# Sines left in PSUM, and a gating whose products run on GpSimd and whose sums run on VectorE in PSUM

## The chip, the cores and the metric

The kernel runs on one core of one Trainium2 chip. A core has five engines with a queue each: TensorE (PE in the profile; its weight loads are shown apart, as PEld), VectorE (DVE), ScalarE (ACT), GpSimd (POOL) and SyncE (SP, which here only issues DMAs). The two on-chip memories are SBUF and PSUM; PSUM is used here as eight banks of 128 x 512 fp32. The metric is the device time of one execution in microseconds (us); lower is better. Everything is fp32.

## The reference

`x` is (1, 2048, 512). Four layers are added to it in turn, A, B, A, B, each on a layer norm of `x` over the channels:

```python
def A(q, k, v, shift_k, ssm_k, ssm_D):            # q is the normalized x
    k_shift = sum(k_pad[:, t:t+S] * shift_k[:, 3-t] for t in range(4))
    kv = k_shift * v                              # the gating: the same in both A layers
    y = causal_conv(kv, ssm_k) + kv * ssm_D       # FFT of length 2S, per channel
    return q * y

def B(u, log_A_real, A_imag, C_real, C_imag, log_dt, D_skip):
    dt = exp(log_dt);  A = -exp(log_A_real) + 1j * A_imag;  C = (C_real + 1j * C_imag) * dt
    K = 2 * real(sum_n C[d, n] * exp(A[d, n] * dt[d] * l))      # the taps, l = 0 .. 2047
    return causal_conv(u, K) + u * D_skip

x = x + A(layernorm(x));  x = x + B(layernorm(x))
x = x + A(layernorm(x));  x = x + B(layernorm(x))
```

`kv` and its convolution don't depend on `x`, so the kernel computes the convolution of A once. It also computes the taps of B once.

## The kernel before

**The stages.** After a short setup (the logarithms, phases and rates of the modes, lines 330 to 424), two generators are run together by `run_steps`: one step of `stream()`, then two of `diagonal()`, again and again.

- `stream()` makes the taps of B (`taps`, 64 steps, four to each of 16 groups of 32 channels) and, behind them, the spectrum of B's filter (`spectrum_quarter(1, ...)`).
- `diagonal()` makes the spectrum of A's filter (four quarters of 12 steps). With each of these steps it runs one step of `kv_steps`, which is the gating: 16 groups of 32 channels, three steps a group, by `gated`. Then it runs the convolution of A (`convolution(0, ...)`), which reads the gated groups back from DRAM (`kv_d`).

When both are done, `gated_update` multiplies `x` by A's result, the first B convolution runs, then the second gated update and the second B convolution. None of these last parts is touched by the change.

**One step of the taps.** A tap is a product of a magnitude and a wave, and each is split into two factors, so that 32 x 64 positions come out of a contraction over the modes.
- `mags` (line 469): TensorE writes log magnitudes to a bank `pm`, ScalarE takes Exp of it into SBUF (L471): `m1` (512 columns a step) and `m2` (512 columns every second step). Twelve Exps are made for eight steps at a time, because Exp and Sin need different activation tables.
- `angles`: TensorE writes a phase in turns into a bank `pa` (L481; there are two such banks), VectorE rounds it (`y`, L485), TensorE subtracts the rounded phase in the same bank (L486).
- `waves`: ScalarE reads `pa` and writes to the SBUF tile `tt` (three of them): the absolute value (L494), the sine (L495), and the cosine from the absolute value (L496).
- `products`, one step later: GpSimd makes L507 (sine and cosine times `m1`, 2 x 8 x 32 columns) and L511 (cosine, 8 x 32 columns). VectorE makes L508 (sine and cosine times `m2`, in place in `tt`, 2 x 8 x 32 columns) and L509 (minus the sine times `m1`, 8 x 32 columns). All operands are in SBUF.
- `contract` (L522): 32 small matmuls add the products up in the bank `pk`; every fourth step VectorE scales the result (L531, L532) and SyncE stores it.

**One group of the gating.** `gated` loads a tile `kvt` (19 rows of k, 16 of v, the four shift weights), and does eight elementwise operations of 128 x 512 on it, all in SBUF: VectorE makes L621, L625, L628, L629, GpSimd L622, L623, L626, L630 (the bits of `KVE`). They form one chain of sums `u`, which goes back and forth between the two engines; `u` is stored to `kv_d` by L631. Group 0 is made on GpSimd alone. The tiles `u` and `tb` share the tags `vv` and `sw` (two buffers each) with the convolution of A.

**PSUM.** In this part of the kernel the eight banks are: one `pk`, two `pa`, two `pm`, and three of the tag `c1`, which the forward transforms (`pf`, L171), the spectrum (`pu`, L196), and the convolution of A (`pi`, `po`) take in turn. The SBUF tag `pc` has two buffers: the spectrum of A copies a bank `pu` there by ScalarE (L247) and stores it to DRAM (L248).

**What sets the order.** The program is written in the order above, but `TileContext(schedule_with_timeline_sim=True)` lets a planner choose the order on each engine when the program is built, from its own modelled times. Each engine then works through its queue in that order and waits where an operand or a buffer isn't ready.

Of the kernel before, what the change touches and what calls it, by code (L numbers as in the profile page):

```python
# [24 lines left out]
TWO_PI = 6.283185  # L25
# [74 lines left out]
def kernel(ctx: ExitStack, tc: tile.TileContext, out, x_in, kv_in, ssmk_in, ssmd_in,  # L100
# [336 lines left out]
    NT = 3  # L437
    tts = []
    for i in range(NT):
        tt = wk.tile([128, 2, 8, 65], F32, name=f"tt{i}")  # L440
        G.memset(tt[:, 0, :, 0], 1.0)
        G.memset(tt[:, 1, :, 0], 0.0)
        tts.append(tt)


    rows, ms, xys, pks, angs = {}, {}, {}, {}, {}
    NXY = 2
    NM1 = 9
    NM2 = 5
    E2P = 1000  # L450
    XLP = 1000
    last_exp, last_sin = [None], [None]
# [11 lines left out]
    def mags(gi, k, col):  # L464
        h, s = divmod(k, 2)
        hs = slice(64 * h, 64 * h + 64)
        pm = pp.tile([128, 512], F32, name="pm", tag="pm", bufs=NPM)
        rhs = tabs["tg2"][hs] if col == 2 else tabs["tg1"][hs, 8 * s:8 * s + 8, :]
        mt = T.matmul(pm, rows[gi][hs, 1, :], rhs, start=True, stop=True)  # L469
        m = wk.tile([128, 512], F32, name=f"m{col}", tag=f"m{col}", bufs=NM2 if col == 2 else NM1)  # L470
        i = S.activation(m, pm, AF.Exp)  # L471
        if last_sin[0] is not None:
            after(i, last_sin[0])
        last_exp[0] = i
        ms[gi, k, col] = m

# [12 lines left out]
    def waves(gi, k):  # L489
        r = angs[gi, k]  # L490
        tt = tts[(4 * gi + k) % NT]
        rv = r.rearrange("p (c i) -> p c i", i=64)
        co = tt[:, 0, :, 1:65]
        S.activation(co, rv, AF.Abs)  # L494
        for i in (S.activation(tt[:, 1, :, 1:65], rv, AF.Sin, scale=TWO_PI),  # L495
                  S.activation(co, co, AF.Sin, scale=-TWO_PI, bias=halfpi)):  # L496
            after(i, last_exp[0])
            last_sin[0] = i

    def products(gi, k):  # L500
        h, s = divmod(k, 2)
        tt = tts[(4 * gi + k) % NT]
        m1 = ms[gi, k, 1].rearrange("p (c i) -> p c i", i=64)
        m2 = ms[gi, 2 * h, 2].rearrange("p (c i) -> p c i", i=32)[:, 8 * s:8 * s + 8, :]
        xy = wk.tile([128, 2, 8, 64], F32, name="xy", tag="xy", bufs=NXY)
        e2 = tt[:, :, :, 33:65]
        G.tensor_mul(xy[:, :, :, 32:64], tt[:, :, :, 1:33], m1[:, :, 32:64][:, None].to_broadcast([128, 2, 8, 32]))  # L507
        (G if (4 * gi + k) % E2P == E2P - 1 else V).tensor_mul(e2, e2, m2[:, None].to_broadcast([128, 2, 8, 32]))  # L508
        V.scalar_tensor_tensor(xy[:, 1, :, 0:32], tt[:, 1, :, 0:32], -1.0, m1[:, :, 0:32],  # L509
                               op0=ALU.mult, op1=ALU.mult)  # L510
        (V if (4 * gi + k) % XLP == XLP - 1 else G).tensor_mul(xy[:, 0, :, 0:32], tt[:, 0, :, 0:32], m1[:, :, 0:32])  # L511
        xys[gi, k] = (xy, e2)

    def contract(gi, k):
        xy, e2 = xys[gi, k]
# [86 lines left out]
    with ExitStack() as actx:  # L602
# [9 lines left out]

        def gated(grp, onpool):
            kvt = ap.tile([128, 39, 32], F32, name="kvt", tag="kab", bufs=NKA)
            nc.sync.dma_start(kvt.rearrange("p t c -> p (t c)"), kv_in[grp])
            u = ap.tile([128, 16, 32], F32, name="u", tag="vv", bufs=NSA)
            tb = ap.tile([128, 16, 32], F32, name="tb", tag="sw", bufs=NSA)
            e = [G if (onpool >> i) & 1 else V for i in range(8)]
            sk = lambda j: kvt[:, 35 + j, :][:, None, :].to_broadcast([128, 16, 32])
            kt = lambda j: kvt[:, j:j + 16, :]  # L620
            e[0].tensor_mul(u, kt(3), sk(0))  # L621
            e[1].tensor_mul(tb, kt(0), sk(3))  # L622
            e[2].tensor_add(u, u, tb)  # L623
            yield
            e[3].tensor_mul(tb, kt(1), sk(2))  # L625
            e[4].tensor_add(u, u, tb)  # L626
            yield
            e[5].tensor_mul(kt(2), kt(2), sk(1))  # L628
            e[6].tensor_add(u, u, kt(2))  # L629
            e[7].tensor_mul(u, u, kt(19))  # L630
            nc.sync.dma_start(kv_d[grp], u.rearrange("p t c -> p (t c)"))  # L631
            yield

        KV0 = 1
        KVE = 0b10010110
        def row_stats(t):
# [4 lines left out]
        def kv_steps():  # L641
            for grp in range(KV0, 16):
                yield from gated(grp, KVE)

# [26 lines left out]
        def diagonal():  # L671
            kvs = kv_steps()
            for q in range(NQ):
                for i, _ in enumerate(spectrum_quarter(0, q, ssmk_in, ap, zlast, ZA, "c1")):
                    if q == 0 and i == 1:
                        for grp in range(KV0):
                            for _ in gated(grp, 255):
                                pass
# [272 lines left out]
```

## Time and profile before

| | |
|---|---|
| device time, median of 3 runs | 789.33 us (789.06 to 796.64) |
| span of the profiled execution | 792.0 us, first to last instruction; a time of its own isn't listed beside it |
| PE, DVE busy over the span | 638.7 us (81%), 605.1 us (76%) |
| POOL, ACT busy over the span | 499.9 us (63%), 482.4 us (61%) |
| first and last gating product L630 | 30.0 us, 229.5 us |
| first and last product L507 of the taps | 71.3 us, 509.2 us |
| mean granted clock of TensorE | 0.882 |

The span falls into five stretches: setup (to about 55 us), taps with gating and A's spectrum (55 to 230), taps with the convolution of A (230 to 430), the last taps with the first gated update (430 to 512), and the B convolutions with the second gated update (from 512). The change touches the first four.

How to read the lines of the profile: a line of a group reads `line engine operation out<-in shape xcount | busy us, mean ns | idle before, and what ended it`. A line of one source line gives `duration ns min/median/max`. A line of the timeline gives the start and the duration in us.

### The profile page before, as it was taken

The page shows a single profiled execution, that of the slowest core. Times are in us where ns is not written, and L with a number is a line of the kernel's source. Part 1 is how long each engine was busy: PE and PEld are TensorE (multiplying, and loading weights), DVE is VectorE, ACT ScalarE, POOL GpSimd, SP SyncE. Part 2 cuts the span into 40 slices and gives each one's busy share as a digit, 9 for nine tenths or more (in the row PEclk, how much of TensorE's full clock was granted, in tenths as well). Part 3 has the DMA queues.
Part 4 walks back from the last instruction along what each step waited for, and adds up shares of the span by engine and source line. Part 5 has one row for each costly group of instructions (what it writes and reads, how often), then busy time and mean ns, then how long its engine had stood idle before and what let it go on. Part 6 is the DMA issues. An engine that isn't in the chain of part 4 may idle for free.

```text
span 792.0 us, 14443 instructions
## 1 busy us (share of the span) xinstructions
PE 638.7 (81%) x5064; PEld 450.9 (57%) x5064; DVE 605.1 (76%) x957; ACT 482.4 (61%) x870; POOL 499.9 (63%) x478
## 2 busy tenths in 40 slices
PE   3368697878779988998989885689779963699996
PEld 2255465546567665766757453476647731376673
DVE  7757979998984769657767849745659889968775
ACT  5035356354448695586686598748746638669572
POOL 4865778776858786665778423315766830488793
PEclk9676599678989999999999976599989995999998
DMA  9677167367457464556473591147977631077782
GB/s 324 199 245 276 44 233 254 114 201 258 135 179 199 130 163 129 146 167 183 113 202 116 156 310 71 27 137 202 241 193 211 161 95 65 1 187 228 197 246 101
DMA packets 80396, 135.47 MB, mean 171 GB/s; under 512 B 8508, under 2 KB 29508, under 8 KB 78788
## 3 DMA queue, kind: packets, MB, share of 16 engines
q1 hardware_dynamic: 79428, 132.13, 55.9%
q0 software_dynamic: 896, 2.43, 1.1%
q8 instruction: 40, 0.66, 0.4%
q14 instruction: 32, 0.26, 0.1%
HBM read 98.87 MB, written 35.65 MB: 170 GB/s over the span
## 4 chain that ended last, share of the span: by engine, by line
PE 27%; DVE 11%; ACT 8%; issue 7%; DMA 5%; POOL 3%; SPq 0%; DVEq 0%; POOLq 0%; ACTq 0%
PE pu L196 9%; PE pf L171 6%; PE pi L293 6%; PE po L314 4%; DMA kab<-spec 3%; DVE x L737 2%; ACT tt L494 1%; DMA spec<-pc 1%; PE pm L469 1%; PE pk L522 1%; DVE w L308 1%; DVE xy L509 1%; DVE vv L281 1%; POOL sw L283 1%; ACT m L471 1%
## 5 line engine op out<-in xcount | busy, mean ns | idle before, releaser
L283 POOL TENSOR_TENSOR sw<-sw,kab 128x512 f32<-128x512 f32 x96 | 125.1, 1309 | 70.2 <-ACT sw L280 57.6
L507 POOL TENSOR_TENSOR xy<-tt,m 128x512 f32<-128x512 f32 x64 | 86.4, 1351 | 71.6 <-ACT tt L496 45.5
L171 PE MATMUL pf<-kk,wz 128*128 128x256 f32 x256 | 89.8, 500 | 36.8 <-POOL kk L239 24.8
L281 DVE TENSOR_TENSOR vv<-pu,kab 128x512 f32<-128x512 f32 x96 | 64.8, 680 | 64.9 <-ACT sw L280 35.9
L293 PE MATMUL pi<-vv,mm 128*128 128x128 f32 x768 | 106.5, 283 | 3.1 <-DVE vv L281 1.6
L284 POOL TENSOR_TENSOR vv<-vv,sw 128x512 f32<-128x512 f32 x76 | 99.5, 1313 | 14.1 <-DVE vv L281 11.0
L293 PEld LDWEIGHTS pi<-vv,mm 128*128 128x128 f32 x768 | 95.8, 195 | 16.7 <-issue 8.6
L279 ACT ACTIVATE sw<-pu 64x512 f32<-64x512 f32 x96 | 57.1, 595 | 72.2 <-PE pu L196 70.4
L171 PEld LDWEIGHTS pf<-kk,wz 128*128 128x128 f32 x256 | 60.0, 249 | 56.9 <-POOL kk L239 27.6
L494 ACT ACTIVATE tt<-pa 128x512 f32<-128x512 f32 x64 | 38.3, 599 | 82.4 <-PE pa L486 73.8
L196 PE MATMUL pu<-x,w 128*128 128x128 f32 x512 | 79.3, 306 | 10.7 <-DVE x L191 9.3
L196 PEld LDWEIGHTS pu<-zu,w 128*128 128x128 f32 x512 | 63.4, 193 | 40.0 <-DVE vv L281 15.8
L196 PEld LDWEIGHTS pu<-x,w 128*128 128x128 f32 x512 | 72.3, 215 | 22.6 <-DVE x L191 12.4
L196 PE MATMUL pu<-zu,w 128*128 128x128 f32 x512 | 73.1, 285 | 10.4 <-DVE vv L281 10.1
L508 DVE TENSOR_TENSOR tt<-tt,m 128x512 f32<-128x512 f32 x64 | 73.3, 1145 | 3.4 <-ACT tt L496 3.1
L247 ACT COPY pc<-pu 128x512 f32<-128x512 f32 x64 | 37.5, 592 | 55.0 <-PE pu L196 35.2
L509 DVE SCALAR_TENSOR_TENSOR xy<-tt,m 128x256 f32<-128x256 f32 x64 | 52.7, 824 | 23.2 <-ACT tt L495 12.3
L471 ACT ACTIVATE m<-pm 128x512 f32<-128x512 f32 x96 | 54.0, 604 | 21.2 <-PE pm L469 20.1
L522 PE MATMUL pk<-xy,tt 128*32 128x64 f32 x2048 | 51.6, 240 | 13.7 <-POOL xy L511 8.1
L314 PE MATMUL po<-w,w 128*64 128x512 f32 x192 | 54.9, 662 | 8.5 <-DVE w L308 6.8
L191 DVE STREAM_TRANSPOSE x<-pf 128x512 f32<-128x512 f32 x64 | 44.8, 704 | 20.3 <-PE pf L171 20.3
L522 PEld LDWEIGHTS pk<-xy,tt 128*32 128x32 f32 x2048 | 38.0, 121 | 38.8 <-issue 16.9
(146 smaller groups left out, 1310.9 us busy)
## 6 DMA issues: line engine op xcount, KB each, us to landing
kab<-spec SPq DMA_DIRECT2D x188, 256.0 KB, 4.0
spec<-pc SPq DMA_DIRECT2D x64, 256.0 KB, 2.1
kvt<-kv_in SPq DMA_DIRECT2D x16, 624.0 KB
yaq<-ya_d SPq DMA_DIRECT2D x8, 1024.0 KB, 7.1
kk<-ssmk_in SPq DMA_DIRECT2D x16, 256.0 KB, 3.1
kv_d<-u SPq DMA_DIRECT2D x16, 256.0 KB, 7.3
kdram<-ks SPq DMA_DIRECT2D x64, 64.0 KB, 1.9
kk<-kdram SPq DMA_DIRECT2D x16, 256.0 KB, 2.9
```

The source lines that it names most:

```text
L171: yield T.matmul(o, w, rhs, start=True, stop=True)
L196: ins = T.matmul(pu[:, i, :], w2[:, c * CK + i, :], z[:, :, c * CK + i, :], start=True, stop=True)
L281: V.tensor_mul(vv, pu, kabs[s][:, 0])
L283: (V if last else G).tensor_mul(sw, sw, kabs[s][:, 1])
L284: (V if last or s % add_dve == add_dve - 1 else G).tensor_add(vv, vv, sw)
L293: i1s[t] = T.matmul(pi[:, i, :], mm[:, c * CK + i, :], vvs[t][:, i, :], start=True, stop=True)
L314: ins = T.matmul(po[64 * a:64 * a + 64], w4, ws[g][:, :, 16 * a:16 * a + 16, :].rearrange("p x t r -> p t x r"), start=True, stop=True, ti ...
L471: i = S.activation(m, pm, AF.Exp)
L507: G.tensor_mul(xy[:, :, :, 32:64], tt[:, :, :, 1:33], m1[:, :, 32:64][:, None].to_broadcast([128, 2, 8, 32]))
L508: (G if (4 * gi + k) % E2P == E2P - 1 else V).tensor_mul(e2, e2, m2[:, None].to_broadcast([128, 2, 8, 32]))
L509: V.scalar_tensor_tensor(xy[:, 1, :, 0:32], tt[:, 1, :, 0:32], -1.0, m1[:, :, 0:32], op0=ALU.mult, op1=ALU.mult)
L522: T.matmul(pk[32 * i4:32 * i4 + 32, 2 * k + i, :], e2[:, r, 4 * i + i4, :], xy[:, r, 4 * i + i4, :], start=r == 0, stop=r == 1, tile_posit ...
```

## The change

**Taps.** The sine is no longer written to SBUF: ScalarE writes it over the phase in the bank `pa`. Only the cosine goes to SBUF, to `co`. The four products become: GpSimd makes both products with the cosine (512 and 256 columns), and VectorE both with the sine, which it reads from PSUM (512 and 248 columns). `m1` and `m2` lie side by side in one tile `m` of 16 x 96 columns, so one product covers a factor with `m1` and one with `m2`. The results go to `xye`, which holds the two factors of the contraction (two tiles, used in turn; its one column that stays zero is set once).

**Gating.** GpSimd makes the four products of shifted k and shift weight (`term`, in the tags `vv` and `sw`). ScalarE copies the first into a bank `acc` of the tag `c1`, VectorE adds the other three to it in PSUM, and multiplies by v into a tile `un`, which takes a buffer of the tag `pc` and is stored from there. Group 0 is made in the same way. The three steps of a group stay three: two products, two products, the rest.

```diff
     def mags(gi, k, col):
-        m = wk.tile([128, 512], F32, name=f"m{col}", tag=f"m{col}", bufs=NM2 if col == 2 else NM1)
-        i = S.activation(m, pm, AF.Exp)
+        if col == 2:
+            ms[gi, h] = wk.tile([128, 16, 96], F32, name="m", tag="m", bufs=NM)     # NM = 5
+            m = ms[gi, h][:, :, 64:96]
+        else:
+            m = ms[gi, h][:, 8 * s:8 * s + 8, 0:64]
+        i = S.activation(m, pm.rearrange("p (c i) -> p c i", c=16 if col == 2 else 8), AF.Exp)
     def waves(gi, k):
+        rv = angs[gi, k].rearrange("p (c i) -> p c i", i=64)
+        co = cosines[(4 * gi + k) % NT][:, :, 1:65]
         S.activation(co, rv, AF.Abs)
-        for i in (S.activation(tt[:, 1, :, 1:65], rv, AF.Sin, scale=TWO_PI),
+        for i in (S.activation(rv, rv, AF.Sin, scale=TWO_PI),
                   S.activation(co, co, AF.Sin, scale=-TWO_PI, bias=halfpi)):
     def products(gi, k):
-        G.tensor_mul(xy[:, :, :, 32:64], tt[:, :, :, 1:33], m1[:, :, 32:64][:, None].to_broadcast([128, 2, 8, 32]))
-        (G if (4 * gi + k) % E2P == E2P - 1 else V).tensor_mul(e2, e2, m2[:, None].to_broadcast([128, 2, 8, 32]))
-        V.scalar_tensor_tensor(xy[:, 1, :, 0:32], tt[:, 1, :, 0:32], -1.0, m1[:, :, 0:32],
-        (V if (4 * gi + k) % XLP == XLP - 1 else G).tensor_mul(xy[:, 0, :, 0:32], tt[:, 0, :, 0:32], m1[:, :, 0:32])
+        si = angs[gi, k].rearrange("p (c i) -> p c i", i=64)
+        co = cosines[(4 * gi + k) % NT]
+        m = ms[gi, h][:, 8 * s:8 * s + 8, :]
+        xye = factors[(4 * gi + k) % NXY]                                           # NXY = 2
+        G.tensor_mul(xye[:, 0, :, 32:96], co[:, :, 1:65], m[:, :, 32:96])
+        V.tensor_mul(xye[:, 1, :, 32:96], si, m[:, :, 32:96])
+        V.scalar_tensor_tensor(xye[:, 1, :, 1:32], si[:, :, 0:31], -1.0, m[:, :, 1:32],
+        G.tensor_mul(xye[:, 0, :, 0:32], co[:, :, 0:32], m[:, :, 0:32])
     def contract(gi, k):
-                    T.matmul(pk[32 * i4:32 * i4 + 32, 2 * k + i, :], e2[:, r, 4 * i + i4, :],
-                             xy[:, r, 4 * i + i4, :], start=r == 0, stop=r == 1,
+                    T.matmul(pk[32 * i4:32 * i4 + 32, 2 * k + i, :], xye[:, r, 4 * i + i4, 64:96],
+                             xye[:, r, 4 * i + i4, 0:64], start=r == 0, stop=r == 1,
...
-        def gated(grp, onpool):
+        def gated(grp):
-            e[0].tensor_mul(u, kt(3), sk(0))
-            e[1].tensor_mul(tb, kt(0), sk(3))
-            e[2].tensor_add(u, u, tb)
-            yield
-            e[3].tensor_mul(tb, kt(1), sk(2))
-            e[4].tensor_add(u, u, tb)
+            for j, tag in enumerate(("vv", "sw", "vv", "sw")):
+                term = ap.tile([128, 16, 32], F32, name="term", tag=tag, bufs=NSA)  # NSA = 2
+                G.tensor_mul(term, kvt[:, 3 - j:19 - j, :], tap(j))
+                terms.append(term)
+                if j == 1:
+                    yield
             yield
-            e[5].tensor_mul(kt(2), kt(2), sk(1))
-            e[6].tensor_add(u, u, kt(2))
-            e[7].tensor_mul(u, u, kt(19))
-            nc.sync.dma_start(kv_d[grp], u.rearrange("p t c -> p (t c)"))
+            acc = bank("acc").rearrange("p (t c) -> p t c", c=32)
+            S.copy(acc, terms[0])
+            for term in terms[1:]:
+                V.tensor_add(acc, acc, term)
+            un = ap.tile([128, 16, 32], F32, name="un", tag="pc", bufs=2)
+            V.tensor_mul(un, acc, kvt[:, 19:35, :])
+            nc.sync.dma_start(kv_d[grp], un.rearrange("p t c -> p (t c)"))
             yield
```

More of the change, by code (lines that the diff above doesn't have):

```diff
@@ L437 @@
     NT = 3
-    tts = []
+    NXY = 2
+    cosines, factors = [], []
     for i in range(NT):
[L440 to L451, printed above, removed]
+        co = wk.tile([128, 8, 65], F32, name=f"co{i}")
+        G.memset(co[:, :, 0], 1.0)
+        cosines.append(co)
+    for i in range(NXY):
+        xye = wk.tile([128, 2, 8, 96], F32, name=f"xye{i}")
+        G.memset(xye[:, 1, :, 0], 0.0)
+        factors.append(xye)
+    rows, ms, pks, angs = {}, {}, {}, {}
+    NM = 5
     last_exp, last_sin = [None], [None]
@@ L501, in products @@
         h, s = divmod(k, 2)
[L502 to L509, printed above, removed]
+        si = angs[gi, k].rearrange("p (c i) -> p c i", i=64)
[5 more added lines that the diff above has]
+        V.scalar_tensor_tensor(xye[:, 1, :, 1:32], si[:, :, 0:31], -1.0, m[:, :, 1:32],
                                op0=ALU.mult, op1=ALU.mult)
-        (V if (4 * gi + k) % XLP == XLP - 1 else G).tensor_mul(xy[:, 0, :, 0:32], tt[:, 0, :, 0:32], m1[:, :, 0:32])
-        xys[gi, k] = (xy, e2)
+        G.tensor_mul(xye[:, 0, :, 0:32], co[:, :, 0:32], m[:, :, 0:32])
     def contract(gi, k):
-        xy, e2 = xys[gi, k]
+        xye = factors[(4 * gi + k) % NXY]
         if k == 0:
@@ L611 @@
         NWA = 1
-        def gated(grp, onpool):
+        def gated(grp):
             kvt = ap.tile([128, 39, 32], F32, name="kvt", tag="kab", bufs=NKA)
             nc.sync.dma_start(kvt.rearrange("p t c -> p (t c)"), kv_in[grp])
[L616 to L623, printed above, removed]
-            yield
-            e[3].tensor_mul(tb, kt(1), sk(2))
-            e[4].tensor_add(u, u, tb)
-            yield
-            e[5].tensor_mul(kt(2), kt(2), sk(1))
-            e[6].tensor_add(u, u, kt(2))
-            e[7].tensor_mul(u, u, kt(19))
-            nc.sync.dma_start(kv_d[grp], u.rearrange("p t c -> p (t c)"))
+            tap = lambda j: kvt[:, 35 + j, :][:, None, :].to_broadcast([128, 16, 32])
+            terms = []
+            for j, tag in enumerate(("vv", "sw", "vv", "sw")):
[4 more added lines that the diff above has]
+                    yield
+            yield
+            acc = bank("acc").rearrange("p (t c) -> p t c", c=32)
[5 more added lines that the diff above has]
+            nc.sync.dma_start(kv_d[grp], un.rearrange("p t c -> p (t c)"))
             yield
         KV0 = 1
-        KVE = 0b10010110
         def row_stats(t):
@@ L642, in kv_steps @@
             for grp in range(KV0, 16):
-                yield from gated(grp, KVE)
+                yield from gated(grp)
         def steps_a(q):
@@ L676, in diagonal @@
                         for grp in range(KV0):
-                            for _ in gated(grp, 255):
+                            for _ in gated(grp):
                                 pass
```

5 lines of the change are left out of this document (removed).

## The prediction

> **What bounds the kernel now.** I read the stages first: the busy time of each engine in the three stretches that hold the taps (columns: PE, PEld, DVE, ACT, POOL, clock, DMA).
>
> ```profile
> core 0: us, PE busy (x) PEld busy (x) DVE busy (x) ACT busy (x) POOL busy (x), PEclk, DMA share, GB/s
> 55.00:230.00 175.00, 143.54 (x1219) 100.18 (x1217) 160.79 (x209) 84.46 (x146) 126.27 (x115) 0.80 0.59 195
> 230.00:430.00 200.00, 181.31 (x1746) 132.55 (x1746) 136.66 (x188) 144.15 (x251) 141.25 (x132) 0.97 0.56 156
> 430.00:512.00 82.00, 58.57 (x607) 36.55 (x605) 63.51 (x115) 61.49 (x109) 33.51 (x33) 0.74 0.42 139
> ```
>
> In the first stretch (taps, gating, A's spectrum) VectorE is busy 160.8 of 175 us, 92%: it sets the pace, and TensorE idles down to a granted clock of 0.80. In the second (taps and A's convolution) TensorE does, at 181.3 of 200 (91%). In the third nothing is full. The chain of waits breaks off early in the second stretch, so I go by occupancy, and look next at what VectorE's time consists of: the operations that the change touches, over the whole run, with one that it doesn't (L281).
>
> ```profile
> L508 DVE TENSOR_TENSOR tt<-tt,m x64: 641/942/4303, 71.7 to 509.1; 128x512 f32<-128x512 f32 x64
> L509 DVE SCALAR_TENSOR_TENSOR xy<-tt,m x64: 372/428/4818, 70.7 to 508.5; 128x256 f32<-128x256 f32 x64
> L281 DVE TENSOR_TENSOR vv<-pu,kab x96: 645/691/694, 235.0 to 776.0; 128x512 f32<-128x512 f32 x96
> ```
>
> L508 takes 0.64 us at best and 4.3 at worst; L281, as long, with one operand in PSUM, never takes more than 0.694. The timeline of GpSimd and that of VectorE over five microseconds show why.
>
> ```profile
> 361.48 1.26 POOL L284 TENSOR_TENSOR vv<-vv,sw 128x512 f32<-128x512 f32 x1
> 362.71 1.19 POOL L507 TENSOR_TENSOR xy<-tt,m 128x512 f32<-128x512 f32 x1
> 363.87 0.68 POOL L511 TENSOR_TENSOR xy<-tt,m 128x256 f32<-128x256 f32 x1
> 364.51 1.17 POOL L507 TENSOR_TENSOR xy<-tt,m 128x512 f32<-128x512 f32 x1
> 365.65 0.68 POOL L511 TENSOR_TENSOR xy<-tt,m 128x256 f32<-128x256 f32 x1
> ```
>
> ```profile
> 361.79 4.82 DVE L509 SCALAR_TENSOR_TENSOR xy<-tt,m 128x256 f32<-128x256 f32 x1 [0.98 <-ACT tt L495]
> 366.54 0.68 DVE L508 TENSOR_TENSOR tt<-tt,m 128x512 f32<-128x512 f32 x1
> ```
>
> A 0.43 us operation with both operands in SBUF stands 4.82 us, until GpSimd's fifth operation in a row has ended, and all of VectorE's queue stands behind it. So much of VectorE's "busy" is being held by GpSimd.
>
> **The change, part by part.** First stretch, VectorE's groups and then GpSimd's:
>
> ```profile
> L508 DVE TENSOR_TENSOR tt<-tt,m 128x512 f32<-128x512 f32 x23 | 30.3, 1318 | 0.0
> L509 DVE SCALAR_TENSOR_TENSOR xy<-tt,m 128x256 f32<-128x256 f32 x24 | 22.6, 940 | 5.8 <-ACT tt L495 5.8
> L191 DVE STREAM_TRANSPOSE x<-pf 128x512 f32<-128x512 f32 x31 | 21.5, 699 | 5.1 <-PE pf L171 5.1
> L628 DVE TENSOR_TENSOR kvt<-kvt 128x512 f32<-128x512 f32 x13 | 16.9, 1298 | 0.0
> L625 DVE TENSOR_TENSOR tb<-kvt 128x512 f32<-128x512 f32 x12 | 16.1, 1339 | 1.2 <-POOL u L623 1.2
> L485 DVE TENSOR_SCALAR y<-pa 128x512 fp32r<-128x512 f32 x23 | 15.3, 668 | 2.0 <-PE pa L481 2.0
> L621 DVE TENSOR_TENSOR u<-kvt 128x512 f32<-128x512 f32 x12 | 15.0, 1247 | 0.0
> L629 DVE TENSOR_TENSOR u<-u,kvt 128x512 f32<-128x512 f32 x13 | 11.6, 890 | 0.0
> ```
>
> ```profile
> L507 POOL TENSOR_TENSOR xy<-tt,m 128x512 f32<-128x512 f32 x24 | 30.4, 1265 | 13.1 <-ACT tt L496 10.9 <-ACT pc L247 1.2 <-DVE tt L508 0.8
> L511 POOL TENSOR_TENSOR xy<-tt,m 128x256 f32<-128x256 f32 x24 | 21.8, 910 | 0.0
> L630 POOL TENSOR_TENSOR u<-u,kvt 128x512 f32<-128x512 f32 x13 | 18.4, 1413 | 14.1 <-DVE u L629 14.1
> L626 POOL TENSOR_TENSOR u<-u,tb 128x512 f32<-128x512 f32 x13 | 18.1, 1389 | 8.7 <-DVE tb L625 8.7
> L623 POOL TENSOR_TENSOR u<-u,tb 128x512 f32<-128x512 f32 x12 | 17.1, 1421 | 9.3 <-issue 5.4 <-DVE u L621 2.5 <-POOL xy L511 0.7
> L622 POOL TENSOR_TENSOR tb<-kvt 128x512 f32<-128x512 f32 x11 | 15.9, 1450 | 0.1
> ```
>
> VectorE loses 30.3 + 22.6 + 16.9 + 16.1 + 15.0 + 11.6 = 112.5 us. It gets 23 sine products at L281's 0.691 = 15.9, 24 short ones at L509's median of 0.428 = 10.3, and for the 50 gating operations 50 adds and products at 0.691 = 34.6: 60.8 in all. So 160.8 - 51.7 = 109.1. Reading PSUM is shown by L281; writing PSUM from VectorE is shown by no row. The adds' bounds are L281's least, 0.645, and L628's mean, 1.298, if they are held after all; I take 0.691, since the operands are L281's. [...] The upper bound would cost 38 adds x 0.61 = 23 us of VectorE. [...] The least of L281 and of L508 differ by 0.004, the medians can't be compared. [...]
>
> GpSimd does as many operations as before, 2 a tap and 4 a group, but unheld, at the medians of three rows:
>
> ```profile
> L507 POOL TENSOR_TENSOR xy<-tt,m x64: 1162/1207/1880, 71.3 to 509.2; 128x512 f32<-128x512 f32 x64
> L511 POOL TENSOR_TENSOR xy<-tt,m x64: 667/745/1145, 72.5 to 510.8; 128x256 f32<-128x256 f32 x64
> L283 POOL TENSOR_TENSOR sw<-sw,kab x96: 1255/1277/1742, 235.1 to 775.7; 128x512 f32<-128x512 f32 x96
> ```
>
> Lost are 121.7 us (the six groups above); added 24 x (1.207 + 0.745) + 49 x 1.277 = 109.4; so 126.3 - 12.3 = 114.0. The 14.1 + 8.7 us in which it waited for VectorE's half of the sum go too: its four products need only `kvt` and free buffers.
>
> ```profile
> L495 ACT ACTIVATE tt<-pa x64: 581/592/619, 70.0 to 507.8; 128x512 f32<-128x512 f32 x64
> L496 ACT ACTIVATE tt<-tt,halfpi x64: 706/723/771, 70.5 to 508.3; 128x512 f32<-128x512 f32 x64
> ```
>
> ScalarE gets 12.5 copies into `acc` at 0.592 = 7.4, so 91.9 us. Its sine now writes PSUM, which no row shows; the two rows differ by 0.13 for the memory read, so I bound it at ±0.13 x 64 = ±8 us of ScalarE over all taps, and take none.
>
> Now the time. The four engines' busy times add up to 515.1 us in 175, so 2.94 are busy at once; in the second stretch 603.4 in 200, 3.02. After the change the first has 109.1 + 91.9 + 114.0 + 143.5 = 458.5: 156 us at 2.94, 152 at 3.02. If TensorE, idling less, is granted 0.97 as in the second stretch, its 143.5 become 118.3 and the stretch 433.3 / 3.02 = 143. I take 150: **25 us less**. Its floor: were TensorE at 0.97 as full as VectorE is now, 118.3 / 0.919 = 129, or 46 less.
>
> Second stretch:
>
> ```profile
> L508 DVE TENSOR_TENSOR tt<-tt,m 128x512 f32<-128x512 f32 x27 | 28.6, 1059 | 1.8 <-ACT tt L496 1.5
> L509 DVE SCALAR_TENSOR_TENSOR xy<-tt,m 128x256 f32<-128x256 f32 x27 | 24.9, 922 | 6.5 <-ACT tt L495 6.5
> ```
>
> 53.5 become 27 x (0.691 + 0.428) = 30.2, so 23.3 less, and (603.4 - 23.3) / 3.02 = 192: **8 us less**. TensorE's idle time, 200 - 181.3 = 18.7, is the most that can go. Third stretch: the last 14 taps at 23.3 / 27 = 0.86 each are 12.1 us of VectorE, with 217.1 / 82 = 2.65 engines busy at once 4.6 us; the sine's longer stay in its bank (below) lies on this sparse stretch's path, so **3 us less**. The setup holds the first groups of the gating, whose products GpSimd now makes without a break; VectorE's setup operations on SBUF may be held once more (4.8 us, the case above) or less; I take none.
>
> New waits. VectorE's adds wait for GpSimd's third and fourth product, with `y` of the next tap and the transposes queued behind; ScalarE's copy waits for the first, with Exp and sine of the next tap behind. They are issued one and two steps of `diagonal` after the products; 24 taps in 175 us are 7.3 us a tap, 3.65 a step, against 2 x 1.277 a step for the products, so this is mostly covered. If the last product is always late by its own length it costs 12.5 x 1.277 = 16 us; I take a quarter, **4 us more**. `acc` takes one of three `c1` banks for some 0.6 + 4 x 0.69 = 3.4 us of every 11; the transforms can go on with two, and I cost it at nothing; without that cover it is part of the 16. At nothing also: the Exps (same number and size), the memsets, TensorE's 32 matmuls (same shapes), `xye` (two tiles, as `xy` had), and the store, which leaves SP when VectorE's product is done and not GpSimd's.
>
> Sum: -25 - 8 - 3 + 4 = -32. The profiled span is 792.0, so 760; the median of the runs is 2.7 below that span, so I forecast **757 us**.
>
> **Rivals.** *TensorE sets the pace at once.* The first stretch's 143.5 us at clock 0.80 are already 82%; at 92% of the time with no better clock the stretch ends at 156, the second, full already, gains nothing, and the total is 792.0 - 19 - 3 - 2.7 = 767. For it: the second stretch. Against: the clock follows the load.
>
> *The angle banks.* The two `pa` banks are now free only after VectorE's two products, not after the sine. TensorE's wait for such a bank (L481) stands in the first row here:
>
> ```profile
>   ACT tt L495: 14.9, 18
>   DMA spec<-pc: 19.5, 11
> ```
>
> If all 18 waits grow by the two products (0.69 + 0.43) and one more operation of VectorE in front (0.69), 18 x 1.8 = 33 us eat the gain: 790; with the products alone (20 us) 777. Against: it was rarely binding, 18 of 64 taps.
>
> *The stores' buffers: slower.* `un` takes one of the two `pc` buffers until its store has landed. These are the landings of the gating's store (L631) and of the spectrum's (L248), and the second row above is ScalarE's present wait for the latter, at L247:
>
> ```profile
> DMA to landing us min/median/max: 2.0/7.3/8.0
> DMA to landing us min/median/max: 2.0/2.1/4.3
> ```
>
> A buffer is held for 0.7 + 7.3 = 8.0 us where a copy held it for some 3, and if the copy behind it must wait it out, 13 groups x (8.0 - 3.65) = 57 us fall on ScalarE, with the sines behind it: 757 + 57 = 814. It turns the sign when some 40 of these 57 come through, that is, when copies follow each other one a step while a store takes over two steps. For it: 11 such waits already. Against: the other buffer turns round in 0.6 + 2.1, and ScalarE idles for 90 of 175 us. That the change doesn't do what it says (adds held at 1.298) costs 23 / 2.94 = 8 us and stays within the forecast's range.
>
> **How the numbers follow.** Forecast 0.57 (its own range 735 to 772), TensorE's pace 0.13, angle banks 0.17, stores 0.13. A measurement can tell about 1%, 8 us. Faster by more: the first two and about a third of the third, 0.76. Within 1%: the rest of the third and a little of the last, 0.12. Slower: 0.12. The range: below, the first stretch's floor in large part and the second's idle time by half (-46 + 4 - 9 - 5 = -56: 733); above, most of the angle banks' case, 787.
>
> **What would show it.** Right: the sine products and adds at 0.64 to 0.70 with no long ones, VectorE near 110 us in the gating's stretch, the last gating product near 205 and the last product of the taps near 477, the clock above 0.85 there. Wrong: L481 waiting for VectorE by over 20 us, L247 waiting for the gating's store, VectorE idle on GpSimd's products, or adds at 1.3.

## The result, and the profile after

The changed kernel takes 764.24 us (median of 4 runs, 758.1 to 766.39) against 789.19 us: a ratio of 0.967, with a 95% interval of 0.962 to 0.971. It is faster, by 25 us of the 32 forecast; 764 lies in the forecast's own range. The profiled execution has a span of 763.3 us and a time of 765.14 (before: span 792.0); TensorE's mean granted clock is 0.895 (before: 0.882). Ratios use fast runs alone; the profiles of two kernels below, the gating's part alone at the old pace (813.77 us) and the changed kernel at pace 3:2 (1130.23 us), fell on slow runs, so these two have no row in the table of chains.

I cut both traces at the same events and not at round times: the first and the 32nd of A's convolution's products on VectorE (L281), and the end of the last product of the taps (L511). These are the stages of the kernel before:

```profile
core 0: us, PE busy (x) PEld busy (x) DVE busy (x) ACT busy (x) POOL busy (x), PEclk, DMA share, GB/s
0.00:235.00 235.00, 170.26 (x1320) 120.91 (x1321) 201.85 (x263) 101.07 (x172) 164.62 (x162) 0.80 0.63 207
235.00:428.50 193.50, 176.50 (x1699) 128.43 (x1698) 132.57 (x182) 142.68 (x248) 139.02 (x130) 0.99 0.56 157
428.50:511.50 83.00, 59.59 (x616) 36.88 (x614) 64.28 (x115) 61.39 (x108) 34.82 (x34) 0.74 0.42 138
511.50:792.00 280.50, 232.38 (x1432) 164.69 (x1432) 206.43 (x399) 177.30 (x342) 161.40 (x154) 0.92 0.59 160
```

And these of the changed kernel, the same columns:

```profile
0.00:215.30 215.30, 161.83 (x1365) 115.51 (x1365) 154.56 (x269) 114.09 (x196) 138.64 (x157) 0.86 0.70 229
215.30:389.60 174.30, 166.48 (x1604) 120.55 (x1602) 109.03 (x170) 133.36 (x232) 124.19 (x124) 0.98 0.61 170
389.60:481.90 92.30, 70.31 (x702) 47.09 (x703) 65.72 (x141) 72.44 (x139) 32.77 (x40) 0.79 0.38 127
481.90:763.30 281.40, 226.38 (x1397) 159.27 (x1396) 199.36 (x381) 167.84 (x318) 159.07 (x153) 0.91 0.57 159
```

| stage | before | after | difference |
|---|---|---|---|
| to the convolution's start (setup, gating, A's spectrum) | 235.0 | 215.3 | -19.7 |
| convolution of A, with taps | 193.5 | 174.3 | -19.2 |
| last taps, with the first update | 83.0 | 92.3 | +9.3 |
| the rest | 280.5 | 281.4 | +0.9 |
| span | 792.0 | 763.3 | -28.7 |

VectorE's busy time falls by 47.3 us in the first stage and by 23.5 in the second. The second and third stage have to be read together: of VectorE's 64 sine products (L508, one a tap), 26 fall into the second stage before and 24 after, 14 and 16 into the third. So two taps' work was pushed back from a full stage to a sparse one, and both together give 9.9 us.

The operations that the change made on VectorE, by source line (duration in ns, least, median and longest):

```profile
L508 DVE TENSOR_TENSOR xye<-pa,m x64: 644/683/694, 65.4 to 477.1; 128x512 f32<-128x512 f32 x64
L509 DVE SCALAR_TENSOR_TENSOR xye<-pa,m x64: 391/405/406, 66.0 to 477.7; 128x248 f32<-128x248 f32 x64
L627 DVE TENSOR_TENSOR acc<-acc,term x48: 659/690/700, 28.3 to 193.6; 128x512 f32<-128x512 f32 x48
L629 DVE TENSOR_TENSOR un<-acc,kvt x16: 651/680/693, 32.5 to 194.3; 128x512 f32<-128x512 f32 x16
```

Not one of 192 is held: the longest takes 0.700 us, where the sine product took up to 4.303 before. The adds both read and write PSUM, which no row of before showed. VectorE is not free of GpSimd altogether, though. The cast of the taps' rows, which the change doesn't touch, has one operand, in SBUF, and writes to SBUF:

```profile
L462 DVE CAST rw<-raw x16: 265/515/3926, 45.7 to 416.9; 128x256 fp32r<-128x256 f32 x16
```

Its longest, 3.926 us from 224.93, ends at 228.86; GpSimd works without a break from 224.96 to 228.70 there (two L283 and one L284). The 16 casts took 8.4 us before and take 13.1 now.

GpSimd's groups over the whole run, in the form of the page's costliest groups, and the row of L507 before under them:

```profile
L619 POOL TENSOR_TENSOR term<-kvt 128x512 f32<-128x512 f32 x64 | 81.6, 1294 | 34.6 <-ACT acc L625 24.5 <-DMA kvt<-kv_in 6.2 <-DVE acc L627 3.6
L507 POOL TENSOR_TENSOR xye<-co,m 128x512 f32<-128x512 f32 x64 | 75.4, 1178 | 57.3 <-issue 32.4 <-ACT co L497 15.9 <-PE pk L521 6.2
```

```profile
L507 POOL TENSOR_TENSOR xy<-tt,m 128x512 f32<-128x512 f32 x64 | 86.4, 1351 | 71.6 <-ACT tt L496 45.5 <-DVE w L308 8.5 <-issue 8.5
```

GpSimd's own operations are shorter too: the mean of L507 was 1.351 us and is now 1.178. The new wait stands in the first row: 24.5 us for ScalarE's copy into `acc`. This is the view of that copy's line (first its durations; then what its engine idled for; then who waited for it):

```profile
L625 ACT COPY acc<-term x16: 579/590/606, 23.6 to 188.2; 128x512 f32<-128x512 f32 x16
...
  DVE x L191: 15.9, 5
  DVE un L629: 6.1, 2
...
  POOL term L619: 24.5, 7
```

The copy waits for one of the three `c1` banks: 15.9 us for VectorE's transpose out of a transform's bank, 6.1 for the bank of the group before, which VectorE's last product releases. That product itself waits 5.1 us for its `pc` buffer (3.2 for a spectrum store, 1.9 for the spectrum's copy, in the view of L629).

### The profile page after: what moved, and what is told of

It is laid out like the page before. It is cut to its first block, busy times and chain, and to the rows that moved or that the text cites. A ratio compares the mean times of both kernels' runs of the same rounds, so it can differ in the third digit from the quotient of the medians.

```text
span 763.3 us, 14414 instructions
## 1 busy us (share of the span) xinstructions
PE 625.0 (82%) x5064; PEld 442.4 (58%) x5064; DVE 528.7 (69%) x961; ACT 487.7 (64%) x884; POOL 454.7 (60%) x473
## 4 chain that ended last, share of the span: by engine, by line
PE 46%; DVE 13%; DMA 12%; ACT 12%; issue 10%; POOL 3%; SPq 2%; ACTq 0%; DVEq 0%; POOLq 0%
PE pu L196 14%; PE pf L171 12%; PE pi L293 7%; PE po L314 4%; DMA kab<-spec 3%; PE pk L521 3%; PE pm L469 3%; PE pa L484 2%; DMA ya_d<-ya 2%; PE pa L489 2%; DMA spec<-pc 2%; ACT m L475 1%; DMA xt<-x_in 1%; DMA rows_d<-hl 1%; DVE x L735 1%
## 5 line engine op out<-in xcount | busy, mean ns | idle before, releaser
L283 POOL TENSOR_TENSOR sw<-sw,kab 128x512 f32<-128x512 f32 x96 | 123.5, 1291 | 72.4 <-ACT sw L280 65.6
L281 DVE TENSOR_TENSOR vv<-pu,kab 128x512 f32<-128x512 f32 x96 | 65.0, 681 | 70.5 <-ACT sw L280 40.2
L171 PE MATMUL pf<-kk,wz 128*128 128x256 f32 x256 | 79.3, 452 | 40.7 <-POOL kk L239 38.2
L507 POOL TENSOR_TENSOR xye<-co,m 128x512 f32<-128x512 f32 x64 | 75.4, 1178 | 57.3 <-issue 32.4
L284 POOL TENSOR_TENSOR vv<-vv,sw 128x512 f32<-128x512 f32 x76 | 98.5, 1298 | 13.1 <-DVE vv L281 9.8
L619 POOL TENSOR_TENSOR term<-kvt 128x512 f32<-128x512 f32 x64 | 81.6, 1294 | 34.6 <-ACT acc L625 24.5
L171 PEld LDWEIGHTS pf<-kk,wz 128*128 128x128 f32 x256 | 53.0, 221 | 57.3 <-POOL kk L239 40.2
L196 PE MATMUL pu<-x,w 128*128 128x128 f32 x512 | 77.6, 298 | 9.5 <-ACT pc L247 3.5
L196 PEld LDWEIGHTS pu<-x,w 128*128 128x128 f32 x512 | 69.2, 206 | 22.3 <-ACT pc L247 5.1
L247 ACT COPY pc<-pu 128x512 f32<-128x512 f32 x64 | 36.8, 588 | 58.5 <-PE pu L196 38.7
L475 ACT ACTIVATE m<-pm 128x512 f32<-128x512 f32 x96 | 54.1, 602 | 22.0 <-PE pm L469 20.7
L495 ACT ACTIVATE co<-pa 128x512 f32<-128x512 f32 x64 | 38.4, 601 | 40.5 <-PE pa L489 40.0
L508 DVE TENSOR_TENSOR xye<-pa,m 128x512 f32<-128x512 f32 x64 | 43.3, 677 | 22.7 <-ACT pa L496 19.3
L521 PE MATMUL pk<-xye 128*32 128x64 f32 x2048 | 52.2, 238 | 7.3 <-POOL xye L511 7.0
L469 PE MATMUL pm<-tg,rw 64*128 64x512 f32 x96 | 45.6, 546 | 14.7 <-ACT m L475 12.2
```

The lines of the kernel that those rows point to most:

```text
L171: yield T.matmul(o, w, rhs, start=True, stop=True)
L196: ins = T.matmul(pu[:, i, :], w2[:, c * CK + i, :], z[:, :, c * CK + i, :], start=True, stop=True)
L281: V.tensor_mul(vv, pu, kabs[s][:, 0])
L283: (V if last else G).tensor_mul(sw, sw, kabs[s][:, 1])
L284: (V if last or s % add_dve == add_dve - 1 else G).tensor_add(vv, vv, sw)
L475: i = S.activation(m, pm.rearrange("p (c i) -> p c i", c=16 if col == 2 else 8), AF.Exp)
```

## The experiments

All kernels compute the whole reference. Ratios are to the kernel before, run on the same chip. For each of them the planner makes the order anew. In the kernels with the sine in SBUF and with the sums in SBUF, VectorE's 961 instructions stand in another order than in the changed kernel, from the 63rd and the 39th on. So the durations of single operations show what an edit does to them; a difference of the whole time is the edit's and the new order's together, and no run here parts the two.

First the table to which the sections refer: where the two chains of the middle end in each profile, in us. One chain is the gating (its last store is issued in the first column), A's convolution and the first gated update; the other is the taps. What follows needs both.

| kernel | last gating store | end of first update | end of taps | span | span after the later of the two |
|---|---|---|---|---|---|
| before | 230.8 | 497.2 | 511.5 | 792.0 | 280.5 |
| after | 195.8 | 446.9 | 481.9 | 763.3 | 281.4 |
| taps' part alone | 219.2 | 473.9 | 509.9 | 791.3 | 281.4 |
| sine in SBUF | 242.2 | 525.6 | 516.2 | 807.0 | 281.4 |
| sums in SBUF | 206.1 | 472.7 | 497.9 | 780.3 | 282.4 |
| before, pace 3:2 | 233.0 | 495.5 | 477.7 | 774.0 | 278.5 |
| taps' part alone, pace 3:2 | 222.0 | 480.2 | 489.2 | 770.1 | 280.9 |
| gating's part alone, pace 3:2 | 233.0 | 516.3 | 466.1 | 794.2 | 277.9 |
| after, update held behind the taps | 192.9 | 477.5 | 459.7 | 756.5 | 279.0 |
| after, own buffers for `un` | 188.5 | 440.6 | 475.0 | 760.7 | 285.7 |
| after, pace 3:2, own buffers | 187.9 | 446.4 | 450.8 | 730.8 | 280.0 |
| the same, update held back | 190.2 | 453.0 | 437.2 | 734.5 | 281.5 |

The last column is 278 to 286 us in all of them: the end follows whichever chain ends later. In the changed kernel the update's chain came 50 us forward and the taps 30, and the update now stands ready 35 us before the taps (481.9 - 446.9), where it was 14 us before.

### Does the memory of the sine matter, or the new split of the products?

The change with the sine written to SBUF again; the same four products on the same engines:

```diff
+    sines = [wk.tile([128, 8, 64], F32, name=f"sn{i}") for i in range(2)]
-        for i in (S.activation(rv, rv, AF.Sin, scale=TWO_PI),
+        for i in (S.activation(sines[k % 2], rv, AF.Sin, scale=TWO_PI),
-        si = angs[gi, k].rearrange("p (c i) -> p c i", i=64)
+        si = sines[k % 2]
```

> The changed kernel, but the sine goes to one of two SBUF tiles and VectorE reads it from there: same operations on the same engines. Holding theory: the sine products are held again, means near 1.1 and 0.8 us with maxima above 3 us, and 10 to 18 us are lost, 774 to 782 us. Rival (it is the new split of the products that counts): 762 to 767 us. Rival (the sine's stay in the two angle banks costs): faster than the changed kernel, 750 to 760 us.

Measured: 806.59 us, ratio 1.017 (1.008 to 1.025). The lines of VectorE's two sine products in this kernel:

```profile
L509 DVE TENSOR_TENSOR xye<-sn,m x64: 642/954/7269, 65.0 to 509.9; 128x512 f32<-128x512 f32 x64
L510 DVE SCALAR_TENSOR_TENSOR xye<-sn,m x64: 402/892/4691, 65.6 to 510.4; 128x248 f32<-128x248 f32 x64
```

Same shapes, same engine, another memory: up to 7.27 us for one of 0.64, and by the ratios (1.017 against 0.967) 39 us more than with the sine in PSUM, which is more than the whole gain of the change. GpSimd works without a break beside that longest product (from 159.44 to 166.35; the product stands from 159.64 to 166.91). That the hold depends on the operand's memory is shown by these durations; the 39 us contain the new order too. Both rivals, with 750 to 767 us, are out. I had the size too small, 10 to 18 us: VectorE's two products take 89.0 + 62.5 us in this kernel and 43.3 + 25.7 in the changed one, 82 us in all, more than the 57 us by which they stood over their free durations before.

### The same question for the gating's sums

```diff
-            acc = bank("acc").rearrange("p (t c) -> p t c", c=32)
+            acc = ap.tile([128, 16, 32], F32, name="acc", tag="acc", bufs=1)
```

> The changed kernel, but the gating's sum is in an SBUF tile instead of a PSUM bank: same operations on the same engines. Holding theory: the adds are held, mean above 1 us, and 5 to 12 us are lost, 769 to 776 us. Rival (the bank that the sum takes from the transforms costs more than the holding): 755 to 763 us, with the waits of ScalarE's copy for a bank (16 us) and of GpSimd for that copy (24 us) gone.

Measured: 781.64 us, ratio 0.986 (0.978 to 0.994). The adds in this kernel:

```profile
L627 DVE TENSOR_TENSOR acc<-acc,term x48: 644/1467/3099, 28.2 to 204.4; 128x512 f32<-128x512 f32 x48
```

69.3 us for the 48 (mean 1.444) where the bank gives 32.9, and 15 us of the time (0.986 against 0.967), more than the 5 to 12 expected. So a bank for the sum is worth its price here, although there are three only, and although the copy into it waits.

### Each part alone

One kernel has only the taps' half of the diff (`mags`, `waves`, `products`, `contract`), the other only the gating's half (`gated`).

> The taps as in the changed kernel, the gating as before. Holding theory (VectorE's operations with two SBUF operands stand still while GpSimd works, and one operand in PSUM frees them): the sine products at 0.64 to 0.70 us with no long ones, the gating's VectorE operations still 0.65 to 2.5 us; of the 25 us about 15 remain, 770 to 778 us. Rival (the gain comes from the gating's chain, which no longer goes back and forth between the two engines): nearly none, 784 to 789 us.

> The gating as in the changed kernel, the taps as before. Holding theory: adds at 0.64 to 0.70 us, L508 and L509 still with maxima above 3 us, about 10 of the 25 us, 774 to 782 us. Rival (the chain of the gating): nearly all of it, 764 to 768 us.

Measured: the taps' part 793.84 us, ratio 1.001 (0.997 to 1.005); the gating's part about 802 us, ratio 1.012 (1.000 to 1.024). I had expected a gain from each. Alone, none gains, and one may lose. VectorE's groups of the gating in the kernel with the taps' part alone, from 0 to 260 us (the lines are one lower than before):

```profile
L627 DVE TENSOR_TENSOR kvt<-kvt 128x512 f32<-128x512 f32 x15 | 25.9, 1724 | 0.1
L508 DVE TENSOR_TENSOR xye<-pa,m 128x512 f32<-128x512 f32 x28 | 19.0, 677 | 12.2 <-ACT pa L496 11.7 <-PE pk L521 0.5
L624 DVE TENSOR_TENSOR tb<-kvt 128x512 f32<-128x512 f32 x15 | 17.9, 1193 | 3.7 <-POOL u L622 3.7
L620 DVE TENSOR_TENSOR u<-kvt 128x512 f32<-128x512 f32 x15 | 16.4, 1096 | 3.1 <-DMA kv_d<-u 2.6 <-POOL u L622 0.5
L628 DVE TENSOR_TENSOR u<-u,kvt 128x512 f32<-128x512 f32 x15 | 11.7, 781 | 0.0
```

The sine products are free (0.677), but the four of the gating take 71.9 us, against 70.8 in the same stretch before: they are held as much as they were. The table shows the rest: the gating ends 12 us earlier (219.2 for 230.8) and the update's chain 23, but the taps only 2, and the taps set the end.

### Where the two chains meet: the pace of the two generators

The table says that the taps end last in the kernel before and after. `run_steps` can give them more steps:

```diff
-        RT = 1
-        RD = 2
+        RT = 2
+        RD = 3
```

> The changed kernel, with three steps of the diagonal to two of the taps instead of two to one. Theory (two chains meet before the B convolutions: A's convolution with the first gated update, and the taps; in the changed kernel the first ends 36 us before the second, so its gain is lost): the taps end earlier, the update later, both near 460 us, and 8 to 18 us are won, 746 to 757 us. Rival (the last batch of taps is a chain of latencies that no pace shortens): 760 to 768 us.

> The kernel before with the same pace, three to two. Theory of the two chains: they end at 491 and 509 us there, so at most half of the 18 us can be won, 780 to 789 us; if it wins as much as the changed kernel does, the pace helps whatever the change, and the theory of the lost gain falls.

Measured: the changed kernel 754.04 us, 0.953 (0.946 to 0.961), as expected; the kernel before 774.60 us, 0.981 (0.975 to 0.987). Both gain, the kernel before by more than I expected: its taps now end at 477.7 and its update at 495.5, so the end moves by about the 16 us between 511.5 and 495.5 and no further. The expectation had named a sign against the theory of a lost gain, that the kernel before wins as much by the pace as the changed one. It wins at least as much: 0.019 (about 15 us), where the changed kernel goes from 0.967 to 0.953 (about 11). So the pace helps whatever the change, and the theory that it gives back a gain which the change had lost falls. What stands is that the later of the two chains sets the end. The change is worth 0.953 against 0.981 at this pace, still some 22 us.

At this pace the two parts alone, to see whether it was only the meeting point that hid their gain:

> The taps' part alone, at the pace of three to two. Theory (in the taps' part alone A's convolution and the first update had ended 20 us earlier than before, and only the last taps hid it): with the pace mended the gain shows, 8 to 16 us under the kernel before at the same pace (774.6), 758 to 767 us. Rival (the taps' part is worth nothing without the gating's): 771 to 778 us.

> The gating's part alone, at the pace of three to two. Theory (GpSimd's four products in a run hold the taps' operations of VectorE longer than the old chain did, so this part alone does harm): 10 to 25 us over the kernel before at that pace, 785 to 800 us, with L509's mean above 1 us. Rival (it was slow only because the two chains met badly): 765 to 775 us.

Measured: the taps' part 770.98 us, 0.980 (0.972 to 0.987); the gating's part 792.01 us, 1.003 (0.999 to 1.007). The first equals the kernel before at this pace (0.981); I had expected 758 to 767, and it is the rival (the taps' part is worth nothing without the gating's) that named this time. Its update ends 15 us earlier than there, its taps 11 later, and why the taps come later I can't say; whether a third pace would show a gain was not tried. The second is a loss of 17 us against that kernel, as expected in size; the mean of L509, expected above 1 us, is 0.907. VectorE's products of the taps over the whole run, in the gating's part alone and then in the kernel before, both at this pace:

```profile
L508 DVE TENSOR_TENSOR tt<-tt,m 128x512 f32<-128x512 f32 x64 | 78.8, 1232 | 2.4 <-ACT tt L496 2.2
L509 DVE SCALAR_TENSOR_TENSOR xy<-tt,m 128x256 f32<-128x256 f32 x64 | 58.0, 907 | 19.2 <-ACT tt L495 18.8 <-PE pk L522 0.4
```

```profile
L508 DVE TENSOR_TENSOR tt<-tt,m 128x512 f32<-128x512 f32 x64 | 79.1, 1237 | 1.7 <-ACT tt L496 1.2
L509 DVE SCALAR_TENSOR_TENSOR xy<-tt,m 128x256 f32<-128x256 f32 x64 | 50.1, 784 | 23.4 <-ACT tt L495 17.3 <-issue 4.9 <-POOL vv L284 0.9
```

The sine's long products take as much in both, the short ones 8 us more. The theory was that GpSimd's four products, which now follow one another with no wait for VectorE's half of the sum, hold VectorE longer. These rows show little of it, and the taps even end 12 us earlier (466.1 for 477.7). The loss lies in the other chain: the gating ends at 233.0 in both, but A's convolution starts at 254.8 and not at 229.8 (first L281), and the update ends at 516.3 and not at 495.5. With its chains 50 us apart, this kernel does not refute the rival that they only met badly. Why A's convolution starts later here stays open.

At this pace, then: neither part 0.981, taps 0.980, gating 1.003, both 0.953. The parts do not add up: each is worth something only beside the other. Why is not shown.

### The last batch of the taps, behind the update

In the changed kernel 24 us lie between the absolute values (L495) of the 58th and the 59th tap (428.6 to 452.2; before 15 us, 459.6 to 475.0); the expectation below counts them as the 56th and the 57th. The timeline of ScalarE there (start, duration, operation):

```profile
428.64 0.57 ACT L495 ACTIVATE co<-pa 128x512 f32<-128x512 f32 x1
429.12 1.06 ACT L475 ACTIVATE m<-pm 128x512 f32<-128x512 f32 x2
430.07 2.55 ACT L724 ACTIVATE ut<-yaq,rs 128x512 f32<-128x512 f32 x4
432.52 1.07 ACT L475 ACTIVATE m<-pm 128x512 f32<-128x512 f32 x2
433.47 2.56 ACT L724 ACTIVATE ut<-yaq,rs 128x512 f32<-128x512 f32 x4
435.92 1.07 ACT L475 ACTIVATE m<-pm 128x512 f32<-128x512 f32 x2
436.88 1.95 ACT L724 ACTIVATE ut<-yaq,rs 128x512 f32<-128x512 f32 x3
...
452.16 0.58 ACT L495 ACTIVATE co<-pa 128x512 f32<-128x512 f32 x1
```

The factors of the first update (`ut`) are free to run, because its chain is early, and stand between the Exps on which the last taps wait; the update's squares (L741) follow them, up to 452. To take the factors out, they were made to wait for the last sine:

```diff
-            S.activation(groups(uts[t]), yas[t // 4][:, :, t % 4, :], AF.Identity, scale=rs[:, t:t + 1], bias=1.0)
+            i = S.activation(groups(uts[t]), yas[t // 4][:, :, t % 4, :], AF.Identity, scale=rs[:, t:t + 1], bias=1.0)
+            if rnd == 0:
+                after(i, last_sin[0])
```

> The changed kernel, but ScalarE's factors of the first gated update are held behind the last sine of the taps. Theory (the update's ScalarE work between the Exps delays the last batch of taps): the 24 us between the 56th and the 57th tap shrink to about 14, the taps end 8 to 12 us earlier, the update now ends last, 757 to 772 us. Rival (the gap is the batch of Exps alone): the gap stays, and the update comes 15 us later, 773 to 785 us.

Measured: 756.86 us, 0.956 (0.947 to 0.964). The timeline of ScalarE at the same place:

```profile
428.10 0.60 ACT L495 ACTIVATE co<-pa 128x512 f32<-128x512 f32 x1 [1.20 <-PE pa L489]
428.76 1.09 ACT L475 ACTIVATE m<-pm 128x512 f32<-128x512 f32 x2
430.24 1.08 ACT L475 ACTIVATE m<-pm 128x512 f32<-128x512 f32 x2 [0.39 <-PE pm L469]
431.72 1.09 ACT L475 ACTIVATE m<-pm 128x512 f32<-128x512 f32 x2 [0.39 <-PE pm L469]
433.19 0.60 ACT L475 ACTIVATE m<-pm 128x512 f32<-128x512 f32 x1 [0.39 <-PE pm L469]
...
441.99 0.60 ACT L495 ACTIVATE co<-pa 128x512 f32<-128x512 f32 x1
```

The last taps end 22 us earlier (459.7; 8 to 12 were expected), the update 31 later (477.5), and now the update sets the end. The span falls by 7 us, of which 4.4 lie between 481.9 and 477.5; the intervals of this kernel and of the changed one overlap (0.947 to 0.964 and 0.962 to 0.971), so the gain is likely and not shown. That the gap shrinks to 14 us (428.1 to 442.0) when the update's work on ScalarE is moved out is shown.

### The wait for the copy and the bank

The gating's result gets buffers of its own, so that it no longer waits for a spectrum store and holds its bank meanwhile:

```diff
-            un = ap.tile([128, 16, 32], F32, name="un", tag="pc", bufs=2)
+            un = ap.tile([128, 16, 32], F32, name="un", tag="un", bufs=2)
```

> The changed kernel, but the gated product has two buffers of its own instead of sharing those of the spectrum's copies. The prediction's rival of the stores: if their landing costs ScalarE's copies their time, 5 us or more are won, under 760 us. Against it, the copies wait only 2 us for such a store in the trace: 761 to 767 us.

> Both parts, pace three to two, own buffers for the gated product. If the two gains add, 754 - 4 = 750 us, 745 to 753. If the store's buffers cost nothing by themselves: 751 to 757 us. By the two chains, the update's end and the last taps lie within 15 us of each other, and the span ends some 285 us after the later one.

> As the run before, and the first update's factors behind the last sine. If the update between the last Exps still delays the taps at this pace: 743 to 750 us. If the update is now the later chain, putting it last delays the end: 755 to 765 us.

Measured: at the old pace 758.65 us, 0.962 (0.956 to 0.967), which can't be told from the change itself (0.962 to 0.971). At pace 3:2 it is 735.54 us, 0.932 (0.925 to 0.940), and with the update held back as well 734.69 us, 0.930 (0.922 to 0.938). Against the pace alone (0.953) that is 17 us, more than either theory gave it. Holding the update back adds nothing, where 743 to 750 or 755 to 765 us had been expected; without it the two chains already meet (446.4 and 450.8). The waits in the copy's line, in the kernel with the pace and its own buffers (L625; first what ScalarE idled for, then who waited):

```profile
  DVE x L191: 14.6, 4
...
  POOL term L619: 8.0, 4
```

The wait for the bank of the group before (6.1 us) is gone, and GpSimd waits 8.0 us for the copy and not 24.5. The wait for the transforms' banks (14.6) stays. At the old pace own buffers take away as much of GpSimd's wait (to 6.4 us) and are worth 4 us by the ratios; why they are worth 17 at this pace is not shown, since the changed kernel with the pace alone has no row in the table. These two kernels are the fastest of the study, by 54 and 55 us against the kernel before.

## Why the prediction was right

**What bounded the kernel.** Right. VectorE was being held by GpSimd, and in PSUM the operands free it: with the sine in SBUF the sine products take 151.5 us of VectorE and not 69.0, and with the sums in SBUF the adds take 69.3 and not 32.9. These kernels are 39 and 15 us longer, new order included.

**Durations on VectorE.** Taken at 0.691 for the sine products and adds; measured 0.677 and 0.687 in the mean, and never near the upper bound of 1.298. The short product, taken at 0.428, takes 0.402. Its least is 0.391 with the sine in PSUM and 0.402 with the sine in SBUF (L510 there), that of the long one 0.644 and 0.642. At their least, then, the products are 0.011 us shorter and 0.002 longer with the sine in PSUM. That the adds would take as long as L281 (0.691), with their output in PSUM too, was my estimate from that row's operands; the runs show it (L627, 0.687 in the mean, at most 0.700). The cast L462, with one SBUF input, is held up to 3.926 us; what sets it apart from the products and adds, no run here shows.

**The first stretch: -25, and +4 for new waits.** Measured to the convolution's start: -19.7, against -21. It came about in another way than I worked it out. The gating itself ended 35 us earlier (195.8 for 230.8), and its last product L629 at 194 and not the 205 I named. The setup, which I had at nothing, isn't where the gating gained: its fifth store goes out at 75.6 us where it went at 69.4, and the sixth at 85.9 for 103.7. But then the forward transforms of A's first quarter were left, and these are TensorE's. The stages' view of the changed kernel between the gating's end and the convolution's start (columns as above):

```profile
195.00:205.00 10.00, 8.62 (x98) 5.92 (x97) 5.44 (x9) 7.18 (x14) 3.84 (x5) 1.00 0.77 249
205.00:215.00 10.00, 9.85 (x78) 7.17 (x77) 4.71 (x7) 5.88 (x12) 0.00 (x0) 1.00 0.61 180
```

TensorE is busy 18.5 of 20 us there, VectorE 10.2. Before, 4.2 us lay between those two events, now 19.5. So 15 of the 35 us went back: the rival of TensorE's pace was true for these 20 us. A division of the summed busy time by a nearly constant number of busy engines gave nearly the right total by averaging over a part that gained more and a part that gained nothing, and that is luck in part. The four engines' busy time in this stage fell from 637.8 to 569.1 us, by 69 (the working, on its own cut: 57 to 82), but 2.64 engines were busy at once after and 2.71 before, where the working held the number or raised it. The new wait was taken at 4 us; the copy's view shows 24.5 us of waiting on GpSimd, of which own buffers for `un` leave 6.4; by the ratios that is worth 4 us, within what the intervals leave open. At nothing I had put the bank for `acc`, with the cover that two banks are enough. That cover was not there: the copy waits 15.9 us for the transforms' bank. What this wait costs was not measured, since it stays with own buffers for `un` (15.8 us at the old pace, 14.6 at pace 3:2); the 17 us at pace 3:2 are what own buffers for `un` gave, new order included.

**The second stretch -8, the third -3.** Together -9.9 measured, -11 predicted. One by one they are wrong: -19.2 and +9.3. The step that failed is "at 2.65 engines busy at once": the third stretch isn't a matter of occupancy. There ScalarE works through the last Exps with the update's factors between them, and the taps that are left wait for it. An earlier update made that worse. That the two misses nearly cancel is luck as far as the forecast goes.

**The sum.** -32 predicted, -28.7 of the span measured. Of the 7 us between forecast and median (757 and 764.2) about half is this; the other half is the step "the median of the runs is 2.7 below that span". After, the median is 0.9 above the span. That one execution of the kernel before lay a little above its median said nothing about an execution of the changed one.

**The signs named.** The last gating product came at 194 and not near 205. VectorE near 110 us in the gating's stretch, the clock above 0.85 and the last product of the taps near 477 came out: VectorE's busy time to the convolution's start fell by 47.3 us (51.7 forecast), the clock is 0.86 and 0.98 in the first two stages, and the last L511 ends at 481.9.

**The rivals.** The median, 764.2, is nearer to the 767 of TensorE's pace than to the forecast's 757, so the time alone does not part the two. The stages speak against it in the main: from 55 us to the convolution's start TensorE is busy 136.1 of 160.3 us, 85% where this rival needs 92% (82% before), its clock there rose from 0.79 to 0.88, which the rival leaves out, and the second and third stage gain 9.9 us where it has 3.

The angle banks and the stores' buffers are answered by two lines of the changed kernel's waits, the first from the matmul into `pa` (now L484), the others from the spectrum's copy L247:

```profile
  DVE xye L509: 14.4, 18
```

```profile
  DMA spec<-pc: 14.9, 9
  DMA kv_d<-un: 1.9, 2
```

TensorE waits for an angle bank as often and about as long as before (14.4 us for 14.9, 18 times in both), only for VectorE's product where it was ScalarE's sine, and 3.9 us once for a sine: hardly anything was added. With the sine in SBUF, where the bank is free at the sine, the kernel was not faster. ScalarE's copy waits 1.9 us for a gating store, not the 57 that this rival had as its price. It saw the scarce buffer, though, and the wrong waiter: it is VectorE's product that waits for `pc` (5.1 us), and the bank of `acc` behind it (6.1 us). That the adds are held was refuted by L627.

**What I did not see.** That the two chains were 14 us apart before (497.2 and 511.5), and that the change would move them by 50 and 30. I had noted that the chain of waits breaks off and went by occupancy; the ends of the two parallel chains stood in the trace and would have shown that a gain in the gating is only worth what the taps gain with it. The forecast's total didn't suffer, because the taps gained 30 too. Nor was it foreseen that each half of the change gains nothing alone (1.001 and 1.012): the sum added the taps' and the gating's savings as if each stood by itself. Two numbers (the pace) and one tag (for `un`) had 27 us more to give, 0.932 against 0.967.

## What to carry to other kernels

Where single VectorE operations take far longer than their best beside a busy GpSimd, look where their operands lie: with one operand in PSUM, all 192 of this change took 0.700 us at most. Do it for all the groups of a stretch before judging it, since here neither half gained alone (1.001 and 1.012 at the old pace, both 0.967), and expect operations that weren't touched, like the cast (up to 3.926 us), to be held still. After a speed-up, look in the trace where parallel chains meet and rebalance their pace; here that helped with and without the change. A result in a scarce bank had better not share its output buffer with a store: own buffers took GpSimd's wait from 24.5 us to 8.0 at most, and at the better pace the time fell by 17 us.

## What the runs showed of the hardware

- VectorE reading and writing the same PSUM bank with a second operand in SBUF takes 0.659 to 0.700 us for 128 x 512 fp32 beside a busy GpSimd, as an operation that only reads PSUM does in the same kernel (0.637 to 0.714, L281).
- One 128 x 512 operation with both operands in SBUF stood 7.27 us beside GpSimd (0.642 at best), through six of its operations in a row. GpSimd's own are lengthened as well: L507 takes 1.178 us in the mean now, took 1.351 before and 1.321 with the gating's part alone at pace 3:2.
- One operand in SBUF is not always few enough: a cast of 128 x 256 from SBUF to SBUF (L462) took up to 3.926 us beside GpSimd in the changed kernel (0.265 at best).
- ScalarE loads an activation table in 1.283 us: in the changed kernel 7 loads stand at the taps' Exps (L475) and 9 at their sines (L496), as many as before (L471, L495, and one more at the cosine, L496).
- ScalarE's sine takes as long into PSUM as into SBUF: 0.592 us in the median both before and after. The bound of 8 us either way that I gave it was not needed.

```profile
L496 ACT ACTIVATE pa<-pa x64: 582/592/617, 64.7 to 476.5; 128x512 f32<-128x512 f32 x64
```
